# Twelve small loads that nobody reads, on two DMA queues of a decode kernel

## The chip, the cores and the metric

The kernel runs on one core of a Trainium2 chip. The metric is the device time of one execution in microseconds. Three runs of the kernel before gave 188.95 us in the median (188.84 to 189.25).

## The reference

One decode step for a batch of two rows, x of 2 x 448 values in bf16. The rows are normalised, and two branches are added to x: attention over the last 4096 positions of a cache of keys and values (16 query heads, 8 key heads, 256 values a head), and a dense layer with the Mish activation.

```python
xn = layernorm(x)
q  = (xn @ wq)                       # 448 -> 16 heads x 256
k, v = k_cache[:, :, -4096:], v_cache[:, :, -4096:]   # 2 x 8 heads x 4096 x 256 each
p  = softmax(q k^T / 16)
A  = (p v) @ wo                      # 4096 -> 448
h  = xn @ w1 + b1                    # 448 -> 1792
B  = (h * tanh(softplus(h))) @ w2    # 1792 -> 448
out = x + A + B
```

Each key and value is used once for two query heads, so the work is mostly reading: 32 MiB of keys, 32 MiB of values and about 10 MiB of weights.

## The kernel before

The order of all instructions is written out by hand. The cache is worked off in four stages (`u`), each with four of the sixteen (batch, key head) pairs on the 128 partitions, 32 partitions to a pair.

A stage has two loads of k and two of v, 4 MiB each, 128 rows of 32 KB. They share a ring of three buffers with wq, w1 and w2 (`kv_pool`). VectorE turns the keys in blocks (`turns`, line 269), TensorE multiplies them with q (`scores`, line 356), ScalarE takes the exponential (line 364), VectorE turns the weights back (line 367), and TensorE sums the values (`values`, line 402; the last 24 rows of the last load in `values_fixed`, line 435). `finish`, `relay` and `mix` normalise and multiply with wo; `dense_in`, `mish` and `dense_out` are the dense layer, whose second half closes the kernel (`add_rows`, line 249). `pace` is TensorE work whose result is not used.

Every load but one is issued by SyncE, in program order: wq in two halves (line 125), the first two loads of k (line 97), b1 (line 129), w1 (line 500), and then k, v (line 105) and wo (line 111) as buffers come free, and w2 in four parts (line 555). ScalarE issues the load of x (line 118). The store of the result is SyncE's last (line 649). GpSimd issues no DMA: it fills constants (lines 134 to 146), `xs` and the four tiles `sp` (line 281), and has nothing to do after that.

The framework sets the waits. Each DMA of SyncE and ScalarE adds to one of eight completion counters, in turn; a DMA whose counter is in use waits until the earlier DMA on it has landed. DMAs of GpSimd have eight counters of their own. At the end of the program (line 675 in the profile) SyncE waits for the last value of every counter in use, two to an instruction, then all engines meet at a barrier, GpSimd clears the counters, and they meet once more.

Of the kernel before, what the change touches and what calls it, by code (L numbers as in the profile page):

```python
# [11 lines left out]
BF16 = mybir.dt.bfloat16  # L12
# [5 lines left out]
def kernel(  # L18
# [13 lines left out]
    nc = tc.nc  # L32
# [42 lines left out]
    consts = ctx.enter_context(tc.tile_pool(name="consts", bufs=1))  # L75
# [18 lines left out]
    def load_k(u, r):  # L94
        t = ring("k")
        src = kview[u][:, s0:, :].rearrange("j (c t) d -> c j (t d)", c=C)
        nc.sync.dma_start(out=t[:], in_=src[:, :, r * RK * KE : (r + 1) * RK * KE])
        k_t[u, r] = t
# [24 lines left out]
    half = NS * HW // 2  # L123
    for lo in (0, half):
        nc.sync.dma_start(out=wq[:, lo : lo + half], in_=wq_in[:, lo : lo + half])
    wq_t = [wq[:, i * HW : (i + 1) * HW] for i in range(NS)]
    load_k(0, 0)
    load_k(0, 1)
# [10 lines left out]
        out=halves[:], in_=ident[0:2, 0:2].unsqueeze(2).to_broadcast([2, 2, Bsz])  # L139
# [5 lines left out]
    for k in range(KU):  # L145
        nc.gpsimd.tensor_copy(
            out=hot[:, k, :, :, :, k],
            in_=ident[:].rearrange("p (q y) -> p y q", y=4).unsqueeze(2)
# [11 lines left out]
        out=rstd[:], in_=mv[:, 1:2], func=ACT.Sqrt, bias=eps_t[:], scale=1.0  # L160
# [4 lines left out]
        out=xn_bf[:],  # L165
# [8 lines left out]
        out=parm[:], in_=ident[:].rearrange("p (a o) -> p o a", o=2), axis=AXIS.X, op=ALU.add  # L174
# [3 lines left out]
        out=jm[:],  # L178
        in_=ident[:].rearrange("p (a j h) -> p j a h", j=J, h=rep),
# [4 lines left out]
        out=jm[:], in0=jm[:], scalar1=-1.0, scalar2=29952.0, op0=ALU.add, op1=ALU.mult  # L184
# [3 lines left out]
        out=mneg[:], in_=jm[:].unsqueeze(1).to_broadcast([P, TH * 8, J])  # L188
    )
    sel = consts.tile([P, 2, NQ], FP32)  # L190
    for x in range(2):
        for w in range(4):
            at = 32 * w + (2 * (w % 2) + x) * NQ
# [3 lines left out]
            else:  # L197
                nc.vector.tensor_tensor(
                    out=sel[:, x, :], in0=sel[:, x, :], in1=src, op=ALU.add
# [16 lines left out]
    for odd in range(2):  # L216
        for half in range(2):
            o = (half + odd) % 2
            nc.vector.tensor_scalar(
                out=xs[:, odd::2, half * Bsz : (half + 1) * Bsz],  # L220
# [56 lines left out]
    for n in range(2):  # L277
        for e in range(2):
            o = n * 64 + e
            sp = consts.tile([P, G, 32], BF16, name=f"sp{n}{e}")  # L280
            nc.gpsimd.tensor_copy(
                out=sp[:],
                in_=ident[:, o : o + 63 : 2].unsqueeze(1).to_broadcast([P, G, 32]),
            )
            spread[n, e] = sp

    def project():
        q_ps = ps_m.tile([P, 512], FP32, tag="m", name="q_ps")
# [391 lines left out]
```

## Time and profile before

| what | value |
|---|---|
| median of three runs | 188.95 us (188.84 to 189.25) |
| span of the profiled execution | 187.3 us |
| the profiled execution's last record (counters cleared after the program) | 189.25 us after the span's start |
| TensorE busy, weight loads | 84.5 us (45%), 37.4 us (20%) |
| VectorE, ScalarE, GpSimd busy | 92.8 us (50%), 12.4 us (7%), 4.7 us (2%) |
| bytes read, mean rate over the span | 77.67 MB, 415 GB/s |
| mean granted TensorE clock | 0.790 of full speed |

The span runs from the first to the last instruction; the time of a run is longer by what lies around it. A whole time of the profiled execution beside its span is not on the page, so the table has its last record instead.

The DMA view gives packets by queue. q1 is SyncE's queue, q10 ScalarE's, q8 and q14 carry instructions. A packet is one row of a transfer or one completion record of 4 bytes. The profile has the sixteen DMA engines only as a mean; the landing records tell how far apart they finish.

Busy shares are averages over the span. What ends a stage is read from the chain of work that ended last and from the waits.

### The profile page before, as it was taken

Reading aid. Unit: us, or ns where it says so; the run is one execution under the profiler, and the core shown is the slowest. Engines: PE = TensorE matmul, PEld = TensorE weight load, DVE = VectorE, ACT = ScalarE, POOL = GpSimd, SP = SyncE. Lnnn points to the kernel's source line nnn. Section 1 sums busy time; section 2 is a strip of 40 time slices with the busy share of each in tenths; the row PEclk is TensorE's granted clock in tenths of the full one; section 3 lists DMA queues with packets and bytes.
Section 4 is the critical chain, followed back from the end, with each engine's and each line's share of the span. In section 5 each row is a group of like instructions: output and inputs, shape, how many; then the busy total and the mean of one; then the engine's idle time right before and its main releaser. Section 6 shows DMA issues by size and latency. Waiting matters only on the chain.

```text
span 187.3 us, 1938 instructions
## 1 busy us (share of the span) xinstructions
PE 84.5 (45%) x847; PEld 37.4 (20%) x847; DVE 92.8 (50%) x93; ACT 12.4 (7%) x26; POOL 4.7 (2%) x16
## 2 busy tenths in 40 slices
PE   0373015893119000882047002881065068789694
PEld 0211002551003000340012000430021023424353
DVE  6704397974792097038940296048920593040100
ACT  3003000101000100110001000110001000210100
POOL 8100000000000000000000000000000000000000
PEclk9999999955557955599558855698559756999999
DMA  6999999999999999999999999999999999999991
GB/s 215 422 483 427 441 406 408 454 444 448 427 434 413 416 436 406 462 448 441 441 434 402 413 441 422 445 444 434 448 427 420 420 427 434 434 422 408 416 403 45
DMA packets 4195, 77.78 MB, mean 415 GB/s; under 512 B 470, under 2 KB 732, under 8 KB 1628
## 3 DMA queue, kind: packets, MB, share of 16 engines
q1 hardware_dynamic: 4184, 77.67, 97.1%
q8 instruction: 6, 0.10, 0.2%
q14 instruction: 1, 0.01, 0.0%
q10 hardware_dynamic: 4, 0.00, 0.0%
HBM read 77.67 MB, written 0.00 MB: 415 GB/s over the span
## 4 chain that ended last, share of the span: by engine, by line
DMA 64%; DVE 15%; PE 15%; issue 3%; ACT 1%; SPq 1%
DMA v<-in_A_v_cache_dram 32%; DMA k<-in_A_k_cache_dram 15%; DVE kt L269 12%; DMA w<-in_B_w_dram 11%; DMA wq<-in_A_wq_dram 6%; PE pv L402 4%; PE sc L356 3%; PE h_ps L519 2%; DVE p L367 1%; PE acc L249 1%; PE q_ps L291 1%; PE dn L380 1%; DVE rec L388 1%; PE o L435 1%; ACT ex L364 1%
## 5 line engine op out<-in xcount | busy, mean ns | idle before, releaser
L269 DVE STREAM_TRANSPOSE kt<-k 128x4096 f32<-128x4096 f32 x16 | 70.0, 4414 | 33.8 <-DMA k<-in_A_k_cache_dram 33.8
L402 PE MATMUL pv<-v,p 128*32 128x512 bf16 x244 | 22.5, 534 | 59.5 <-DMA v<-in_A_v_cache_dram 59.5
L356 PE MATMUL sc<-kt,qd 128*32 128x512 bf16 x256 | 19.8, 440 | 13.3 <-DVE kt L269 13.3
L402 PEld LDWEIGHTS <-p 128*32 128x32 bf16 x244 | 8.7, 125 | 72.9 <-issue 49.6
L575 PE MATMUL pace<-mneg,ident 128*128 128x512 bf16 x42 | 12.7, 440 | 0.0
L356 PEld LDWEIGHTS <-qd 128*32 128x32 bf16 x256 | 7.1, 104 | 23.5 <-issue 17.5
L447 DVE TENSOR_TENSOR oT<-o,rec 128x16 bf16<-128x16 f32 x4 | 0.7, 174 | 21.3 <-PE o L420 17.6
L367 DVE STREAM_TRANSPOSE p<-ex 128x512 bf16<-128x512 bf16 x8 | 5.2, 690 | 10.8 <-ACT ex L364 10.8
L364 ACT ACTIVATE ex<-sc 128x512 bf16<-128x512 f32 x8 | 4.8, 597 | 86.7 <-PE sc L356 86.7
L388 DVE TENSOR_REDUCE rec<-dn 128x8 f32<-128x512 f32 x4 | 2.8, 691 | 13.3 <-PE dn L380 13.3
L575 PEld LDWEIGHTS <-ident 128*128 128x128 bf16 x43 | 4.2, 111 | 15.1 <-DVE kt L269 9.2
L414 ACT COPY vs<-pv 128x512 f32<-128x512 f32 x4 | 2.3, 586 | 59.5 <-PE pv L402 59.5
L482 PE MATMUL early<-wo,ox 128*2 128x448 bf16 x24 | 5.0, 352 | 1.9 <-ACT ox L473 1.9
L420 PE MATMUL o<-sel,vs 128*128 128x8 f32 x32 | 4.3, 262 | 2.1 <-ACT vs L414 2.1
L420 PEld LDWEIGHTS o<-sel,vs 128*128 128x128 f32 x32 | 4.2, 196 | 4.5 <-ACT vs L414 4.4
L380 PE MATMUL dn<-p,ones 128*128 128x512 bf16 x8 | 2.8, 440 | 3.8 <-DVE p L338 3.8
L575 PE MATMUL pace<-kt,ident 128*128 128x512 bf16 x1 | 0.6, 607 | 8.7 <-DVE kt L269 8.7
L291 PE MATMUL q_ps<-wq,xs 128*32 128x512 bf16 x28 | 3.8, 624 | 1.4 <-DMA wq<-in_A_wq_dram 1.1
L211 PE MATMUL xr_ps<-ident,xrows 2*128 2x2 bf16 x7 | 1.0, 181 | 7.2 <-DVE xrows L210 7.2
L519 PE MATMUL h_ps<-xs,w 128*128 128x4 bf16 x49 | 3.7, 196 | 0.9 <-DMA w<-in_B_w_dram 0.9
L308 DVE COPY qT<-qt_ps 128x16 bf16<-128x16 bf16 x4 | 0.4, 166 | 6.3 <-PE qt_ps L303 6.3
L345 PE MATMUL sc<-mneg,ident 128*128 128x512 bf16 x8 | 3.5, 434 | 0.0
(71 smaller groups left out, 51.7 us busy)
## 6 DMA issues: line engine op xcount, KB each, us to landing
k<-in_A_k_cache_dram SPq DMA_DIRECT2D x8, 4096.0 KB, 27.7
v<-in_A_v_cache_dram SPq DMA_DIRECT2D x7, 4096.0 KB, 21.2
wq<-in_A_wq_dram SPq DMA_DIRECT2D x2, 1792.0 KB, 8.8
wo<-in_A_wo_dram SPq DMA_DIRECT2D x4, 896.0 KB, 19.0
v<-in_A_v_cache_dram SPq DMA_DIRECT2D x1, 2560.0 KB
w<-in_B_w_dram SPq DMA_DIRECT2D x1, 1568.0 KB, 21.2
v<-in_A_v_cache_dram SPq DMA_DIRECT2D x1, 1024.0 KB, 22.2
w<-in_B_w_dram SPq DMA_DIRECT2D x1, 784.0 KB, 23.5
```

What stands on the lines that cost most here:

```text
L269: nc.vector.transpose(out=kt[i][:, :, r, :, :], in_=t[:, r * KE : (r + 1) * KE].bitcast(FP32).rearrange("p (a c j) -> p a c j", c=P // (R ...
L291: nc.tensor.matmul(q_ps[32 * u : 32 * (u + 1), :], lhsT=xs[:, s, :], rhs=wq_t[s][:, u * 512 : (u + 1) * 512], start=(s == 0), stop=(s == N ...
L356: nc.tensor.matmul(sc[32 * w : 32 * (w + 1)].rearrange("p t c m -> p t (c m)"), lhsT=qd[:, u, 2 * n + e, :, :].rearrange("p g q -> p (g q) ...
L364: nc.scalar.activation(out=ex[:, :, :, i, :], in_=sc[:], func=ACT.Exp, scale=scale)
L367: nc.vector.transpose(out=p_all[:, :, h * TH : (h + 1) * TH, :].rearrange("p g t q -> p t g q"), in_=ex[:, h * TH : (h + 1) * TH].rearrang ...
L380: nc.tensor.matmul(dn[:].rearrange("p a q -> p (a q)"), lhsT=ones[:], rhs=p_run[:, i].rearrange("p t q -> p (t q)"), start=(i == 0), stop= ...
L388: nc.vector.tensor_reduce(out=rec[:], in_=dn[:].rearrange("p a q -> p q a"), axis=AXIS.X, op=ALU.add)
L402: nc.tensor.matmul(pv[32 * w : 32 * (w + 1), :, :].rearrange("p x d -> p (x d)"), lhsT=p_run[:, g, 4 * a : 4 * a + 4, :].rearrange("p t q ...
L420: nc.tensor.matmul(po[:, c, :], lhsT=sb[:, x, c::2], rhs=sel[:, x, :], start=(x == 0 and c == 0), stop=(last and x == 1), skip_group_check ...
L482: nc.tensor.matmul(early[:], lhsT=ox[:, i, :], rhs=w[:, i, :], start=False, stop=(u == U - 2 and i == 7),)
L519: nc.tensor.matmul(h_ps[:, i, :, :].rearrange("p k b -> p (k b)"), lhsT=w1_v[:, s, i, :], rhs=xs[:, s, 0 : 2 * Bsz], start=False, stop=(s ...
L575: nc.tensor.matmul(ps[:].rearrange("p t c m -> p (t c m)"), lhsT=ident[:], rhs=rhs, start=True, stop=True, skip_group_check=True,)
```

## The change

A scratch tile `marks` of 16 partitions is added. SyncE loads the first 2, 4, 8 and 12 rows of wo into it, after the two halves of wq and before the first load of k. GpSimd issues eight loads of two rows of wo each, after its last constant. Each load has its own row length, from 256 to 344 values (512 to 688 bytes), and its own place in the tile. Nothing reads the tile.

```diff
     for lo in (0, half):
         nc.sync.dma_start(out=wq[:, lo : lo + half], in_=wq_in[:, lo : lo + half])
+    marks = consts.tile([16, 12, 384], BF16)
+
+    def mark(queue, at, n):
+        w = 256 + 8 * at
+        queue.dma_start(out=marks[0:n, at, 0:w], in_=A_wo[0:n, 0:w])
+
+    for at, n in enumerate((2, 4, 8, 12)):
+        mark(nc.sync, at, n)
     wq_t = [wq[:, i * HW : (i + 1) * HW] for i in range(NS)]
     load_k(0, 0)
...
             spread[n, e] = sp
+
+    for at in range(4, 12):
+        mark(nc.gpsimd, at, 2)
 
     def project():
```

By the built program, the order of the other instructions on every engine stays as it was. The DMAs from the first load of k on take the completion counter four places further in the turn of eight, so the second load of k waits for the landing of x and the load of b1 for that of the first half of wq. The closing waits of SyncE grow from five instructions to nine, because GpSimd's eight counters are now in use; the store's counter, in the fifth and last of them before, is in the fifth of nine.

## The prediction

> **What bounds the kernel now.** I read the DMA view first, then the busy times by stage, the chain of work that ended last, SyncE's waits, and the closing waits of the program (line 675).
>
> ```profile
> DMA  6999999999999999999999999999999999999991
> ...
> q1 hardware_dynamic: 4184, 77.67, 97.1%
> q8 instruction: 6, 0.10, 0.2%
> ...
> q10 hardware_dynamic: 4, 0.00, 0.0%
> ```
>
> Nearly all bytes go over SyncE's queue q1, and the engines are busy in every slice. Six instruction fetches (q8) share them: 0.2% of 16 engines over 187.3 us is 6.0 us, so 1.0 us each, on one engine at a time.
>
> ```profile
> 4.00:12.00 8.00, 3.42 (x26) 1.37 (x30) 4.21 (x25) 0.00 (x0) 1.33 (x6) 1.00 1.03 438
> 12.00:40.00 28.00, 12.53 (x118) 6.67 (x118) 19.57 (x13) 2.66 (x4) 0.00 (x0) 0.96 1.00 433
> ...
> 80.00:160.00 80.00, 32.55 (x320) 12.59 (x319) 41.29 (x24) 4.00 (x10) 0.00 (x0) 0.72 1.01 433
> ...
> 182.00:183.00 1.00, 1.00 (x16) 0.60 (x16) 0.18 (x1) 0.17 (x1) 0.00 (x0) 1.00 0.79 299
> 183.00:184.00 1.00, 1.00 (x26) 0.88 (x24) 0.00 (x0) 0.00 (x0) 0.00 (x0) 1.00 0.36 133
> ```
>
> The last two columns are DMA share and GB/s. The share is 1.00 from 4 us on: the transfers are the bound, and the queue never runs dry. At the end the share falls in steps (0.79, 0.36), since the sixteen engines do not finish together: the completion records of the last weight load lie between 182.64 and 184.59 us.
>
> ```profile
> 157.27 22.25 DMA v<-in_A_v_cache_dram
> 179.51 0.05 issue
> 179.56 0.96 PE o L435 x32
> ...
> 182.41 1.93 PE acc L249 x38
> 184.35 0.02 issue
> 184.37 0.57 PE acc L249 x6
> 184.94 0.37 DVE res L646
> ```
>
> The chain's last stretch: a load of v lands at 179.51, TensorE follows with no slack, the last weights arrive as it needs them (184.59), and the result is ready at 185.3. So a delay of the *slowest* DMA engine moves the end one for one; a delay of a faster one does not.
>
> ```profile
> SPq L649 <- DVE res L646: 16.3, 1, 16.3
> ...
> SPq L675 <- DMA out_dram<-res: 0.6, 1, 0.6
> ```
> ```profile
> L675 SPq EVENT_SEMAPHORE  x4: 28/28/28, 185.7 to 185.9; - x4
> ```
> ```profile
> L675 SPq EVENT_SEMAPHORE  x1: 28/28/28, 186.5 to 186.5; - x1
> ```
>
> After issuing the store of the result (185.37), SyncE runs five waiting instructions, each for two counters. Four pass at once from 185.7 to 185.9, while the store is under way; the fifth holds the store's own counter, waits 0.6 us and passes at 186.5. What follows it (barrier, clearing of counters) ends the span at 187.3.
>
> **The sum's base.** All durations are of the one profiled execution, span 187.3 us. The runs' median is 188.95, 1.65 us more, which is work around the span that the change does not touch; I add the change to 188.95.
>
> **The change part by part.** It removes no work and moves no compute instruction: the order on TensorE, VectorE and ScalarE is the same. It adds twelve loads that nobody reads.
>
> *SyncE's four loads are issued after the two loads of wq, ahead of k.* Issuing a small load took 0.28 us (the store), 0.49 (b1) and 0.53 (x, on ScalarE): four take 1.1 to 2.1, I take 2.0. The two k loads, issued from 1.65 to 2.9, move to about 3.7 to 4.9. The engines are working off wq until its second half lands at 11.88, so 7 us of cover remain: cost nothing. With the cover gone it would cost the 2.0 in full.
>
> *Completion counters.* SyncE and ScalarE's DMAs take eight counters in turn, and a DMA waits for the one eight places before it. Four more DMAs rotate everything from k on by four places. By the built program the second k load now waits for x (landed at 2.0, issue at about 4.3: no wait), and b1's load waits for the first half of wq. That half landed at about 7.6 (the median of the two wq loads is 8.8 and the second took 10.70, so the first took 6.9 from 0.73). Behind b1 on SyncE stands the load of w1, which waits for q_ps until 13.84 anyway; b1 itself is read at 33.9 and sits behind k in the queue (31.3) either way. All later waits name the DMA that they named before. Cost nothing.
>
> *The closing waits: the term I count on.* The same rotation moves the store's counter from the last place to the fifth of nine, since GpSimd's eight counters are added, and their pairing leaves four waiting instructions behind it. The four ahead still pass under the store (185.7 to about 185.95, against 186.5). The four behind are all satisfied, but each has to be run after the store has landed. Four starts from 185.7 to 185.9 are three steps in 0.2 us, 0.065 each: 4 x 0.065 = 0.26 us, on the path. Bounds: 4 x 0.028 (the instruction's own duration) = 0.11, and 4 x 0.07 = 0.28. I take 0.26, because the starts show the full spacing. The clearing of counters that follows (0.096 us for 12) now covers 20: 0 to 0.06, I take 0.03.
>
> *The added transfers.* 26 rows from SyncE (14.2 KB) and 16 from GpSimd (10.1 KB). The trace's packet records give 41 ns for a packet of 896 bytes and 9 ns for a 4-byte completion record. Rows of 512 to 688 bytes lie between; by size 25 to 33 ns. The 470 packets under 512 bytes are 29 large loads with 16 records each and three two-row transfers with 2 each, so a small load uses one engine a row. An engine then gets up to four SyncE rows, 4 x (28 + 9) = 0.15 us, or none, and GpSimd's rows, one each if spread: 32 + 9 = 0.04, with up to eight records 0.10. So 0.04 to 0.25 by engine. Only the slowest engines count. The two that carried b1's rows (and that, if small loads start at the same engines, get most of SyncE's) pass through the middle of the field all along (the records of b1 follow theirs of k), 1 to 1.7 us ahead of the engines that a fetch has held up. I take a middling engine: 1.6 rows x 37 + 41 to 104 ns = 0.10 to 0.16, so 0.13.
>
> The page "DMA: Bandwidth & Descriptors" of the Trainium skill, section "Why a DMA increments its semaphore by 16 and not by 1", says that a load issued from GpSimd posts a completion on all 16 engines whatever its shape. SyncE's two-row b1 posted only 2, so this trace can't show it; by the rule the GpSimd part is 0.10 per engine, by the SyncE row 0.04.
>
> *GpSimd's eight issues.* GpSimd ends its last copy at 5.3 us and does nothing afterwards; no wait follows its loads but the closing ones. No row prices such an issue; the nearest are the issues on the other queues, 0.28 to 0.53, and the copies there, 0.26: eight take 2 to 4 us, done by 10. GpSimd has 175 us to spare.
>
> Sum: 0.26 + 0.03 + 0.13 = 0.42 us, 188.95 + 0.42 = 189.37, rounded to **189.4**, 0.2% up.
>
> **The rivals.** The bound below which this kernel can't be told from no change is 0.2%, 0.38 us; the forecast lies just over it.
>
> *Not slower: the terms stay under the bound.* If the closing waits cost their own duration only (0.11) and the slowest engines get GpSimd's single rows (0.04), the sum is 0.15: 189.1. For it: four satisfied waits may run closer than at 185.7, where the issue of the store stood before them, and engines held up by fetches lead the field by more than any row. It decides as soon as the sum stays under 0.38; against it, the spacing of the waits is read from the same instructions.
>
> *Slower by more: GpSimd's loads hold up something.* VectorE prepares q meanwhile (sel, xrows, xs from 5.5 to 8.9). A delay there has 1.0 us until wq lands (8.9 and 1.9 of matmuls against 11.88), then 3.7 (qd ready at 17.83, k landing at 21.55), then 4.6 before the queue runs dry (w1 lands at 35.0, the next k load was issued at 30.38): 9 us in all. The eight issues as priced stay far inside it. What could reach the stream is a packet of the new queue that stalls its engine for a whole small-load latency, 1.3 us (x: issued at 0.73, landed at 2.03), on an engine that is late: 188.95 + 0.29 + 1.3 = 190.5; half of it, 189.9. Against it: ScalarE's small load shared the engines with wq and its share is 0.0%.
>
> The page "SBUF — State Buffer", section "SBUF: two separate sides", says that a GpSimd operation and some VectorE operations exclude each other on a shared port, for the whole instruction. With about 1 us for each GpSimd issue (the DMA page's first-byte figure) VectorE would lose at most 8 us by this estimate, inside the cover, and the sum stays the same.
>
> *Faster: the late engines change.* The v load that the chain ends with has completion records at 179.24, 179.30 and 179.51. If the added rows shift which engine takes a fetch, the last may fall back on the others: -0.2 to -0.3 on the stream, and with the closing waits at their low bound 188.95 - 0.3 + 0.15 = 188.8. It needs more than 0.38 + 0.29 of gain to be counted as faster; nothing in the profile shows that much.
>
> **How the numbers follow.** Forecast 0.55, under the bound 0.24, GpSimd's loads hold up the stream 0.13, late engines change 0.08. The forecast's terms spread from 0.26 to 0.6; three quarters of it lie above 0.38 (0.42), the rest below (0.13). Slower: 0.42 + 0.13 = 0.55; same: 0.13 + 0.24 = 0.37; faster: 0.08. The range goes from the low end of the faster rival, 188.8, to 190.1, which takes in the milder half of the stall.
>
> **What would show it.** Right: nine waiting instructions at the end of SyncE, the store's wait in the fifth, and 0.25 us from it to the barrier; the chain's landings of v and w no more than 0.25 later; DMA share 1.00 throughout; k issued two microseconds later with wq still landing near 11.9; VectorE's first kt transposes still waiting for k at about 21.6. Wrong: a landing more than 0.5 later, a dip of the DMA share, a wait for GpSimd on any engine, a granted clock under 1.00 in the last 20 us, or a new instruction fetch.

## The result and the profile after

The changed kernel takes 190.11 us, median of five runs (189.73 to 190.38), against 188.95 for the kernel before (188.80 to 189.25) on the same chip. The ratio is 1.0055, 95% interval 1.0037 to 1.0073: slower by 1.04 us by the ratio (0.70 to 1.38), 1.16 by the medians. The forecast was 189.4, and the median lies 0.01 above the upper end of its range. The sign was right; the size was less than half of what came.

The profiled execution of the changed kernel is its quickest run, 189.73 us with a span of 187.9. Wherever a run's time and span are both known, they lie about 1.8 us apart (1.7 to 2.0), before and after, so nothing changed around the span, and the profiled execution of the kernel before (span 187.3) was one of about 189.1. The two traces therefore differ by only 0.6 us, and what follows is read from that smaller difference.

The DMA view of the changed kernel:

```profile
DMA  6999999999999998999999999999999999999990
...
DMA packets 4503, 77.80 MB, mean 414 GB/s; under 512 B 736, under 2 KB 1040, under 8 KB 1936
...
q1 hardware_dynamic: 4236, 77.68, 96.8%
q8 instruction: 6, 0.10, 0.2%
q0 software_dynamic: 256, 0.01, 0.1%
```

A new queue, q0, is GpSimd's. Its eight loads hold 16 rows, but it moved 256 packets: 16 rows and 240 records of 4 bytes. SyncE's q1 has 52 packets more, 26 rows and 26 records. The instruction fetches (q8) are six as before. There is one 8 in the row of the sixteen engines' busy share, near 73 us; at the length of a slice (4.7 us) it can't be told from a 9 that just fell short, and no landing moves there.

The busy times by stage (DMA share and GB/s at the end of each line):

```profile
4.00:12.00 8.00, 3.34 (x22) 1.30 (x23) 3.76 (x23) 0.00 (x0) 5.81 (x14) 1.00 1.05 441
12.00:40.00 28.00, 11.92 (x116) 6.62 (x115) 18.95 (x12) 2.52 (x4) 0.00 (x0) 1.00 1.01 429
...
80.00:160.00 80.00, 39.61 (x324) 15.09 (x324) 41.29 (x24) 3.99 (x10) 0.00 (x0) 0.68 1.00 432
182.00:183.00 1.00, 1.00 (x18) 0.55 (x19) 0.18 (x1) 0.17 (x1) 0.00 (x0) 1.00 0.94 367
183.00:184.00 1.00, 1.00 (x28) 0.90 (x23) 0.00 (x0) 0.00 (x0) 0.00 (x0) 1.00 0.48 183
```

The steady part, 80 to 160 us, moves 432 GB/s against 433: nothing is lost there. 12 to 40 us moves 429 against 433, which over 28 us is 0.26 us of transfer. At the end the engines finish later (share 0.94 and 0.48 where it was 0.79 and 0.36).

The last steps of the chain of work that ended last:

```profile
157.60 22.07 DMA v<-in_A_v_cache_dram
...
179.72 0.96 PE o L446 x32
...
182.72 2.50 PE acc L257 x44
185.22 0.37 DVE res L657
```

It is the same chain, 0.16 us later at the last long load of v (179.67 for 179.51) and 0.28 later at the result, because the last weights land at 184.87 instead of 184.59. The rest of the 0.6 us comes after the result, in the closing instructions (line 686 here, 675 before):

```profile
L686 SPq EVENT_SEMAPHORE  x4: 28/28/28, 186.0 to 186.2; - x4
...
L686 SPq EVENT_SEMAPHORE  x5: 28/28/28, 186.8 to 187.1; - x5
L686 SPq DRAIN  x2: 7/10/13, 187.1 to 187.2; - x2
...
L686 POOLq EVENT_SEMAPHORE_RANGE_CLEAR  x1: 139/139/139, 187.5 to 187.5; - x1
```

Four waits pass while the store is under way. The fifth holds the store's counter, and four more follow it, 0.06 us each: from the store's wait to the drain it is 0.306 us (186.809 to 187.115) where it was 0.065, so 0.24 us on the path. The clearing of the counters took 139 ns, 96 before, and the drain of GpSimd's queue around it 102, 77 before. From the issue of the store to the end of the span it is 0.31 us more.

How the stream came to be later is seen in two views. The timelines of VectorE and SyncE, where the first two transposes of k end and the next load of k is issued, of the kernel before:

```profile
21.58 8.77 DVE L269 STREAM_TRANSPOSE kt<-k 128x4096 f32<-128x4096 f32 x2 [3.75 <-DMA k<-in_A_k_cache_dram]
...
30.38 0.55 SPq L97 DMA_DIRECT2D k<-in_A_k_cache_dram  x1
```

and of the changed kernel:

```profile
22.26 8.77 DVE L277 STREAM_TRANSPOSE kt<-k 128x4096 f32<-128x4096 f32 x2 [4.23 <-DMA k<-in_A_k_cache_dram]
...
31.06 0.55 SPq L97 DMA_DIRECT2D k<-in_A_k_cache_dram  x1
```

The last engine delivers the first k at 22.24 instead of 21.55; VectorE starts 0.68 later and takes as long; the load of k that waits for it is issued 0.68 later. Now the stage from 34 to 38 us, where the loads issued earlier end and this load takes over. Before:

```profile
34.00:38.00 4.00, 3.10 (x42) 2.88 (x41) 4.00 (x2) 0.60 (x1) 0.00 (x0) 1.00 1.09 468
38.00:160.00 122.00, 49.20 (x474) 19.47 (x473) 64.78 (x41) 5.97 (x14) 0.00 (x0) 0.68 1.00 432
```

After:

```profile
34.00:38.00 4.00, 3.10 (x38) 2.31 (x32) 4.00 (x2) 0.60 (x1) 0.00 (x0) 1.00 1.05 434
38.00:160.00 122.00, 56.47 (x483) 22.28 (x481) 65.40 (x41) 5.96 (x14) 0.00 (x0) 0.68 1.00 432
```

468 GB/s became 434, though the share is still above 1.00 (1.05): the engines hold packets, and the packets take longer. By the packet records a packet of 32 KB takes 1.213 us; of those that start between 34 and 36 us some of the changed kernel's take up to 1.62, 2.2 us more in all over the sixteen engines, none in the kernel before. (The rate of so short a stretch is a sign and no measure: kernels without a loss here show 468 to 504. The size is read from the landings.) By the landing records, averaged over the sixteen engines, the load of w1 lands 0.29 us later than before, and the k load behind it 0.56 later. So half of that delay arises at this one place, 10 us after the small loads are done, and from there it stays to 160 us (0.44 to 0.58); the other half is there before, with the first k 0.42 late in the mean. What puts it there is the question of the experiments.

### The profile page after: what moved, and what is told of

Its sections match the earlier page's. It is cut to its first block, busy times and chain, and to the rows that moved or that the text cites. A ratio compares the mean times of both kernels' runs of the same rounds, so it can differ in the third digit from the quotient of the medians.

```text
span 187.9 us, 1954 instructions
## 1 busy us (share of the span) xinstructions
PE 91.3 (49%) x847; PEld 39.6 (21%) x847; DVE 92.3 (49%) x93; ACT 12.4 (7%) x26; POOL 9.1 (5%) x24
## 4 chain that ended last, share of the span: by engine, by line
DMA 63%; PE 16%; DVE 15%; issue 3%; ACT 1%; SPq 1%
DMA v<-in_A_v_cache_dram 31%; DMA k<-in_A_k_cache_dram 15%; DVE kt L277 12%; DMA w<-in_B_w_dram 12%; DMA wq<-in_A_wq_dram 6%; PE pv L413 4%; PE sc L367 3%; PE h_ps L530 2%; DVE p L378 1%; PE acc L257 1%; PE q_ps L302 1%; PE o L431 1%; PE dn L391 1%; PE o L446 1%; DVE rec L399 1%
## 5 line engine op out<-in xcount | busy, mean ns | idle before, releaser
L413 PE MATMUL pv<-v,p 128*32 128x512 bf16 x244 | 23.1, 544 | 53.4 <-DMA v<-in_A_v_cache_dram 53.4
L367 PE MATMUL sc<-kt,qd 128*32 128x512 bf16 x256 | 22.0, 484 | 13.8 <-DVE kt L277 13.8
L367 PEld LDWEIGHTS <-qd 128*32 128x32 bf16 x256 | 7.6, 113 | 26.8 <-issue 22.0
L586 PE MATMUL pace<-mneg,ident 128*128 128x512 bf16 x42 | 12.1, 424 | 0.0
L493 PE MATMUL early<-wo,ox 128*2 128x448 bf16 x24 | 6.5, 426 | 1.9 <-ACT ox L484 1.9
L431 PE MATMUL o<-sel,vs 128*128 128x8 f32 x32 | 5.9, 311 | 2.1 <-ACT vs L425 2.1
L431 PEld LDWEIGHTS o<-sel,vs 128*128 128x128 f32 x32 | 5.7, 261 | 4.5 <-ACT vs L425 4.4
L391 PE MATMUL dn<-p,ones 128*128 128x512 bf16 x8 | 3.3, 499 | 3.4 <-DVE p L349 3.4
L356 PE MATMUL sc<-mneg,ident 128*128 128x512 bf16 x8 | 4.5, 568 | 0.0
L130 POOL DMA_DIRECT2D marks<-in_A_wo_dram x8 | 4.3, 542 | 0.0
## 6 DMA issues: line engine op xcount, KB each, us to landing
w<-in_B_w_dram SPq DMA_DIRECT2D x1, 1568.0 KB, 21.6
w<-in_B_w_dram SPq DMA_DIRECT2D x1, 784.0 KB, 23.8
```

The source lines that it names most:

```text
L367: nc.tensor.matmul(sc[32 * w : 32 * (w + 1)].rearrange("p t c m -> p t (c m)"), lhsT=qd[:, u, 2 * n + e, :, :].rearrange("p g q -> p (g q) ...
L391: nc.tensor.matmul(dn[:].rearrange("p a q -> p (a q)"), lhsT=ones[:], rhs=p_run[:, i].rearrange("p t q -> p (t q)"), start=(i == 0), stop= ...
L413: nc.tensor.matmul(pv[32 * w : 32 * (w + 1), :, :].rearrange("p x d -> p (x d)"), lhsT=p_run[:, g, 4 * a : 4 * a + 4, :].rearrange("p t q ...
L431: nc.tensor.matmul(po[:, c, :], lhsT=sb[:, x, c::2], rhs=sel[:, x, :], start=(x == 0 and c == 0), stop=(last and x == 1), skip_group_check ...
L493: nc.tensor.matmul(early[:], lhsT=ox[:, i, :], rhs=w[:, i, :], start=False, stop=(u == U - 2 and i == 7),)
L586: nc.tensor.matmul(ps[:].rearrange("p t c m -> p (t c m)"), lhsT=ident[:], rhs=rhs, start=True, stop=True, skip_group_check=True,)
```

## The experiments

Each kernel was timed in turns with the kernel before on the same chip, five rounds; the ratio is to that, with its 95% interval. "Field" is the mean landing over the sixteen engines, "next k" the load issued at 30.38 us in the kernel before.

**A copy of the kernel before** (e0). 188.94 us, ratio 1.001 [0.999, 1.003]. Its expectation:

> The kernel before, run once more as a measure of the spread and of what lies between span and time. Both theories: ratio 1.000 within 0.002; spans 186.9 to 187.6 us; time minus span about 1.65 us (the changed kernel's five runs have 1.77 to 1.83). If time minus span is 1.8 here too, the 0.15 between the two kernels outside the span is chance.

Its profiled execution happened to be one of its longer runs, 189.77 us. There the first k landed at 22.02, the next k was issued at 30.84, and 34 to 38 us moved 420 GB/s: the same picture as after the change, with no small load in the kernel. So the kernel before meets this in at least one of its own runs.

**SyncE's four alone** (e1):

```diff
-    for at in range(4, 12):
-        mark(nc.gpsimd, at, 2)
```

> SyncE's four loads alone; GpSimd's eight are left out. The store's counter now stands in the first of five closing waits, with four behind it. Theory A (closing waits plus GpSimd's packets): the store passes in the first wait and the drain follows 0.25 us later than before, landings of the large loads shift by 0.05 us on average, in all +0.30 us, ratio 1.0016. Theory B (SyncE's rows and the later issue of k delay the stream): landings +0.4, in all +0.65, ratio 1.0035.

189.30 us, 1.0026 [1.0015, 1.0037]: +0.49 us by the ratio, and +0.33 by the medians. The interval holds both expectations (1.0016 and 1.0035), so the time does not tell them apart; the profile has to. Its closing waits:

```profile
L684 SPq EVENT_SEMAPHORE  x5: 28/28/28, 186.1 to 186.3; - x5
L684 SPq DRAIN  x2: 7/10/13, 186.4 to 186.4; - x2
```

All five come after the store, since the turn of the counters puts the store's into the first of them: 0.32 us from its passing to the drain (186.06 to 186.38), against 0.065 before. The clearing takes 96 ns as before. The first k landed at 21.78, the next k was issued at 30.60, the field of w1 (34.68) and of the next k (44.46) is within 0.05 us of before. The closing waits make 0.26 us of the rise. In this profile SyncE's rows cost the stream next to nothing; but it is of the quickest of twelve runs (188.92), and what the other 0.1 to 0.2 us of the median is, no profile shows.

**GpSimd's eight alone** (e2):

```diff
-    for at, n in enumerate((2, 4, 8, 12)):
-        mark(nc.sync, at, n)
```

> GpSimd's eight loads alone; SyncE's four are left out. Nine closing waits, the store's counter in the last: nothing behind it. Theory A: no change from the store's landing to the drain, +0.04 for the clearing of 20 counters instead of 12, landings of the large loads +0.4 to +0.5 on average from 44 us on, in all +0.5 to +0.7, ratio 1.003 to 1.004. Theory B: landings +0.05, ratio 1.0005.

189.95 us, 1.0054 [1.0042, 1.0067], as slow as the whole change and slower than either view expected. The profile is of its longest run (190.27). Its closing waits, the last of nine and what follows:

```profile
L684 SPq EVENT_SEMAPHORE  x1: 28/28/28, 187.6 to 187.6; - x1
L684 SPq DRAIN  x2: 7/7/7, 187.7 to 187.7; - x2
```

Here the store's counter is last, so no wait is left behind it, and the end costs 0.07 us at most. The rise lies in the stream:

```profile
34.00:38.00 4.00, 3.29 (x41) 2.52 (x36) 4.00 (x2) 0.60 (x1) 0.00 (x0) 1.00 1.00 396
```

The first k landed at 22.19, the next k was issued at 31.02, and the stage moved 396 GB/s (468 before). From w1 to the next k the field took 10.31 us, 9.76 before. So GpSimd's loads bring the delay of the stream. SyncE's shift the store's counter ahead of other waits, and so bring the delay at the end.

**SyncE's four issued twice** (e3), to double their price:

```diff
+    for at, n in enumerate((2, 4, 8, 12)):
+        mark(nc.sync, 12 + at, n)
```

> The changed kernel with SyncE's four loads issued twice (into other places of the tile), so that the counters turn by eight and the store's counter is again in the last of nine closing waits. Theory A: 0.25 us less than the changed kernel at the end, 0.06 more for the four extra loads: about 0.2 us under it, ratio 1.0045 to the kernel before. Theory B: the rows cost twice, landings +0.8 to +0.9, ratio 1.006 or more.

193.13 us, 1.0244 [1.0205, 1.0284]. Nobody expected this. SyncE's waits and its timeline:

```profile
SPq L130 <- DMA wq<-in_A_wq_dram: 8.4, 2, 4.5
```
```profile
1.66 10.94 SPq L130 DMA_DIRECT2D marks<-in_A_wo_dram  x8
12.64 1.27 SPq L97 DMA_DIRECT2D k<-in_A_k_cache_dram  x2
```

The seventh and eighth small loads take the completion counters of the two wq loads and wait until these have landed; k stands behind them and is issued at 12.64 instead of 3.00. The stage then ran dry:

```profile
12.00:16.00 4.00, 2.50 (x18) 0.83 (x17) 0.42 (x4) 1.73 (x2) 0.00 (x0) 1.00 0.58 199
```

Every later landing is about 3.7 us late. The experiment says nothing of the rows' price. It does show what the turn of eight counters costs when a load falls on one that is still under way. In the change itself that place falls to the load of b1, behind both loads of k.

**More and fewer of GpSimd's packets** (e4, e5). Sixteen of its loads in place of eight, and one load of 16 rows with SyncE's four removed:

```diff
-    for at in range(4, 12):
+    for at in range(4, 20):
```

> The changed kernel with sixteen loads by GpSimd instead of eight. Theory C: k's first landing sees the same eight or so before it, the second eight lie behind it and add 0.1 us of packets: ratio 1.0055 to 1.007. Theory D: GpSimd's share doubles, ratio 1.009 to 1.010.

```diff
-    for at in range(4, 12):
-        mark(nc.gpsimd, at, 2)
+    nc.gpsimd.dma_start(out=marks[0:16, 4, 0:288], in_=A_wo[0:16, 0:288])
```

> Nothing of SyncE's four; GpSimd issues one load of sixteen rows instead of eight of two rows: as many rows, one completion per engine instead of eight. Theory C with the cost by number of packets: 32 packets instead of 256, k's first landing and the later issue as in the kernel before, ratio 1.000 to 1.001. Theory D with a cost for the mere use of the queue: 1.003 or more.

Sixteen loads: 190.08 us, 1.0053 [1.0041, 1.0065], no more than eight; the next k was issued at 31.05, as with eight. One load: 189.04, 1.0008 [0.9995, 1.002], no change that can be told. So the cost of the whole does not grow from eight loads to sixteen, as it would if each packet took its own share of the path. The landing records show how: with sixteen the field of w1 is later itself (35.15 us, 34.94 with eight), so that at the issue of the next k more of it was left, and the next k landed at 45.00, as with eight (44.97). The two delays did not add up there. The profile of the one load is of its longest run (190.11 us), in which the next k was issued at 30.91.

**The issue of k made late by other means** (f3). The kernel before, without any small load; two copies on VectorE between the first two transposes (0.84 us together):

```diff
+            if (u, i, r) == (0, 0, 1):
+                for n in range(2):
+                    nc.vector.tensor_copy(
+                        out=hold[:], in_=jm[:].unsqueeze(1).to_broadcast([P, TH * 8, J])
+                    )
```

> The kernel before with two copies of 0.46 us each on VectorE between the first two turns of the first keys; no load and no wait is added. Every buffer release by these turns, and so the issue of the first load of k after w1, comes 0.92 us later (31.3 instead of 30.4 us). Theory C: rate dips between 34 and 38 us, all later landings 0.7 to 1.2 us later, ratio 1.004 to 1.006. Theory D: w1 lands at 35.0, so a load issued at 31.3 is still ahead of it by 3.7 us: ratio 1.000.

190.26 us, 1.0060 [1.0043, 1.0077]. The issue of k and its stage:

```profile
31.41 0.55 SPq L97 DMA_DIRECT2D k<-in_A_k_cache_dram  x1
```
```profile
34.00:38.00 4.00, 3.77 (x46) 2.74 (x39) 4.00 (x2) 0.60 (x1) 0.00 (x0) 1.00 1.08 435
```

Every load up to w1 landed as before (field within 0.01); the k load issued 1.0 us later landed 0.35 later in the field and 1.14 later on its last engine, with packets of 32 KB 3.1 us too long in all between 34 and 36 us. That is as much as the whole change costs, made by a late issue alone, if by a later one (1.0 us against 0.68). When k was issued, w1 still had 3.2 us to run in the field.

**The same late issue with other work queued ahead** (f4), and that work alone (f1): the first load of wo goes right behind w1, and is left out at its own place.

```diff
+    load_wo(0)
...
-        load_wo(u)
+        if u > 0:
+            load_wo(u)
```

> The two copies on VectorE and the early load of wo together. Theory C: k is issued at 31.3, but the queue now holds 2.1 us more ahead of it, so the delay is covered: no dip, ratio 0.998 to 1.001. Theory D: 1.000. If the delay costs here too, what it costs is not the queue running out but VectorE's own work.

> The kernel before with the first load of wo (0.9 MB, 2.1 us of the queue) issued right behind w1 instead of behind the second load of v; nothing added. Theory C (the loss of the changed kernel comes where w1 ends and the next load of k was issued late: the engines run out of reads although the load was issued some 4 us ahead): k is now issued with 2 us more cover, landings of k 2.1 us later and all else as before, ratio 0.998 to 1.000, fewer runs above 189.3 us. Theory D (GpSimd's packets themselves or the late engines cost it): 1.000.

f4: 189.00 us, 1.0014 [0.9993, 1.0034], with k issued at 31.45, as late as in f3:

```profile
34.00:38.00 4.00, 3.88 (x48) 2.85 (x41) 4.00 (x2) 0.60 (x1) 0.00 (x0) 1.00 1.18 504
```

f1: 189.05 us, 1.0005 [0.9993, 1.0016]. With the issue late, the work queued ahead takes the loss away; without a late issue it gains nothing. f3, f4 and f1 ran on one chip, and the intervals of f3 and f4 don't meet. So this loss is one of a queue that has too little ahead when the next load is issued.

**The same cover in the changed kernel** (f2):

> The changed kernel with the same early load of wo. Theory C: the loss at the end of w1 goes (0.3 to 0.5 us); what stays are the closing waits 0.26, the clearing of counters 0.07 and the packets 0.1 to 0.3, in all 0.4 to 0.6 us over the kernel before, ratio 1.002 to 1.003. Theory D: 1.0055 as without the early load.

189.43 us, 1.0036 [1.0015, 1.0057]; by the medians 0.45 us over before, and 0.68 less than the changed kernel without it, which was timed on another chip. The issue of k (31.15) is as late as after the change, and the stage is whole:

```profile
34.00:38.00 4.00, 3.09 (x38) 2.21 (x32) 4.00 (x2) 0.60 (x1) 0.00 (x0) 1.00 1.16 494
```

Four of its twelve runs took 190.3 to 191.0, so that its interval is wide and overlaps that of the changed kernel: f2 agrees with f3 and f4, and would not settle it without them. Its profile is of one of the four (190.26), and shows the same loss at a second place. A load of v, issued at 95.60 us in the kernel before, comes much later in f2:

```profile
95.60 0.54 SPq L105 DMA_DIRECT2D v<-in_A_v_cache_dram  x1
```
```profile
102.17 0.54 SPq L105 DMA_DIRECT2D v<-in_A_v_cache_dram  x1
```

The load of k ahead of it then had 3.03 us to run in the field, and the v behind took 10.00 us. In g2 below (profile of a run of 190.44 us) it was 3.31 and 10.24. In the twelve other profiles 4.08 us or more were left there (9.31 in the kernel before), and the v took 9.67 to 9.70. The load waits for two transposes on VectorE, which began at 93.42 instead of 86.86; why they did is not shown.

**GpSimd's eight loads later** (g1), alone, held behind a copy of `act_bf` on GpSimd, so that they are issued from 41.6 us on instead of 5.5:

```diff
+    hold = consts.tile([P, NI, 2, Bsz], BF16)
+    nc.gpsimd.tensor_copy(out=hold[:], in_=act_bf[:])
+    for at in range(4, 12):
+        mark(nc.gpsimd, at, 2)
```

> GpSimd's eight loads alone, as in the run without SyncE's four, but held back on GpSimd by one small copy that reads the dense layer's activations, so that they start after 41 us, when the first load of k behind w1 has long been issued. Theory C (their cost is that they make k's first landing, and with it that issue, late): issue at 30.4 to 30.8, no dip from 34 to 38 us; what stays is the clearing of 20 counters, 0.07, and 0.1 for the packets, ratio 1.001. Theory D (the use of GpSimd's queue costs, whenever it is): 1.004 to 1.0055.

189.12 us, 1.0003 [0.9982, 1.0023]; against e2's interval (1.0042 to 1.0067) the same eight loads at another time bring no change that can be told. The first k landed at 21.72, the next k was issued at 30.54:

```profile
34.00:38.00 4.00, 3.09 (x42) 2.79 (x40) 4.00 (x2) 0.60 (x1) 0.00 (x0) 1.00 1.14 490
```

**The store's counter put last** (g2): f2 with four more of SyncE's small loads behind wo, so that the turn of the counters ends with the store's in the ninth wait.

> The changed kernel with the early load of wo and four more small loads of SyncE behind it, so that the counters turn by eight and the store's counter is again in the last of nine closing waits. Both theories: 0.065 us from the store's wait to the drain instead of 0.31, so 0.25 us under the changed kernel with the early load, plus 0.06 for the new rows: about 0.2 under it, ratio to the kernel before 1.0015 to 1.002.

189.10 us, 1.0024 [1.0004, 1.0044]; the median is 0.33 under f2's (on another chip), though the four loads were added. Its last wait and what follows it:

```profile
L690 SPq EVENT_SEMAPHORE  x1: 28/28/28, 187.8 to 187.8; - x1
L690 SPq DRAIN  x2: 7/10/13, 187.9 to 187.9; - x2
```

From the store's wait to the drain it is 0.065 us (187.789 to 187.854), in f2 0.306 (187.340 to 187.646). The intervals of the two ratios overlap (four of the twelve runs of each were over 190), so the 0.24 us is shown by the traces, and the medians only agree with it.

## Why the prediction was right in sign and wrong in size

| Term | predicted | shown by |
|---|---|---|
| closing waits behind the store | 0.26 us | 0.24 in the profile after; e1, g2 |
| clearing of 20 counters | 0.03 | 0.07 (clear +43 ns, drain +25) |
| the stream of transfers | 0.13 | 0.28 in the profile after, its quickest run; 1.04 - 0.31 = about 0.7 over the runs; e2, f3, f4 |
| issue of SyncE's four, turn of counters | 0 | no wait in the profile after; e1 leaves 0.1 to 0.2 open |

*The closing waits: right.* Nine waits, the store's in the fifth, four behind it at 0.06 us. e1, where the turn of the counters sets four behind the store for another reason, shows the same size.

*The clearing: low by 0.04*, above the 0.06 that was given as its upper bound. The bound counted the clearing instruction alone; the drain of GpSimd's queue next to it grew as well.

*SyncE's issues and the rotated counters: right, as far as the profile shows.* From the timeline of SyncE, and its wait for b1's counter:

```profile
1.65 1.31 SPq L130 DMA_DIRECT2D marks<-in_A_wo_dram  x4
3.00 1.25 SPq L97 DMA_DIRECT2D k<-in_A_k_cache_dram  x2
```
```profile
SPq L137 <- DMA wq<-in_A_wq_dram: 3.5, 1, 3.5
```

Four issues took 1.31 us, not 2.0; k followed at 3.00, under wq, which landed at 12.08. b1 waited 3.5 us for the first half of wq, and w1 behind it was issued at 14.05 anyway (13.84 before).

*The added transfers: this step failed*, and in it the sentence on cover: a delay of VectorE "has 1.0 us until wq lands ..., then 3.7 ..., then 4.6 before the queue runs dry (w1 lands at 35.0, the next k load was issued at 30.38): 9 us in all". The first two figures are not in dispute, but they cover VectorE and not k: a first k that lands late itself has only the last of the three. And the 4.6 us was taken as slack, as if a load might be issued until the moment the queue ends. The runs show it isn't. Ordered by the time from the issue of the next k to the field's landing of w1, for all kernels that have only w1 ahead of it:

| kernel | issue of next k, us | lead to w1, us | from w1 to next k in the field, us |
|---|---|---|---|
| e3, SyncE's eight | 34.01 | 4.30 | 9.82 |
| before | 30.38 | 4.26 | 9.76 |
| e4, sixteen of GpSimd's | 31.05 | 4.10 | 9.85 |
| e1, SyncE's four | 30.60 | 4.08 | 9.78 |
| g1, GpSimd's late | 30.54 | 4.07 | 9.76 |
| after | 31.06 | 3.88 | 10.03 |
| e0, long run of a copy of before | 30.84 | 3.85 | 10.13 |
| e5, one of GpSimd's, its longest run | 30.91 | 3.83 | 9.90 |
| e2, GpSimd's eight | 31.02 | 3.75 | 10.31 |
| f3, late by VectorE | 31.41 | 3.24 | 10.11 |

With a lead of 4.07 us or more at most 0.09 us is lost in the field, with 3.88 or less 0.14 to 0.55, and on the last engine more (1.14 in f3, 1.50 in e2). The size does not follow the lead evenly; each row is one execution. The second place, with f2 and g2, has the same border: 3.03 and 3.31 us lost 0.33 and 0.57, and 4.08 or more at most 0.03. So the 4.26 us of the kernel before, taken to the field, held some 0.2 to 0.4 us of cover, and not the 4.6.

The small packets were priced rightly one by one: nearly all rows have 27 to 34 ns in the packet records and every 4-byte record of GpSimd's queue 9, priced at 25 to 33 and 9. But there were more records than priced, and in the field they came to more than 0.13 us: w1 was 0.29 us late after the change (0.12 in e2, 0.03 in e1). And they made the slowest engine's part of the first k late: 22.19 to 22.33 us in four profiles with GpSimd's eight or sixteen loads early, and 22.76 in g2, where kernels without small loads of GpSimd before it have 21.55 to 21.83 (e0's long run 22.02, e3 with its late k left out). VectorE waits for that slowest engine, so the chain ran: late last engine, late transposes, late issue, thin queue. The prediction priced only the first link, and called the others covered.

*That only the slowest engine counts: right at the end, and misleading here.* It matters at every load that an engine waits for, and here the wait set an issue that all sixteen engines need.

*GpSimd's records: the higher of the two figures was nearer.* The page "DMA: Bandwidth & Descriptors" of the Trainium skill, section "Why a DMA increments its semaphore by 16 and not by 1", has a completion on all sixteen engines for a load from GpSimd. The 256 packets of q0 agree: 30 records of 4 bytes a load. Sixteen of them fit the completions; the fourteen others are as many as the engines without a row (e5's one load of sixteen rows has sixteen records). That is 15 records an engine and not the eight that were priced.

*No delay of VectorE by GpSimd's issues: right.*

```profile
5.54 4.27 POOL L130 DMA_DIRECT2D marks<-in_A_wo_dram  x8
```

Eight issues took 4.27 us, 0.54 each, while VectorE prepared q; its last step for that (xs) began at 7.78 us, 8.26 before. The port that the page "SBUF — State Buffer" of the Trainium skill, section "SBUF: two separate sides", describes as shared did not show here.

*The rivals.* "Slower by more" gave 189.9 to 190.5 and the time falls there, but its mechanism did not happen: no packet stalled its engine for 1.3 us, and the longest small row of the profile after took 0.14. That the range reached to 190.1, and so almost to the time, came from half of that stall: the nearness is luck. The rival's other half, a late VectorE, did happen, through the late k and not through GpSimd's issues, and was set aside by the 9 us of cover. "Under the bound" fell with the spacing of the closing waits. "Late engines change" is not seen: the last long load of v landed 0.16 us later, not earlier.

*The signs.* Nine waits, the time from the store's wait and wq near 11.9 (12.08) came as named, and the end of the chain nearly so (0.16 and 0.28 later, for at most 0.25). The first kt transposes did not (22.26 for 21.6), and one of the signs of being wrong came: landings more than 0.5 us later, 0.69 at the first k and 0.56 in the field of the next. It points at the step that failed.

*What stays open.* Why the lead has to be about 4 us was not shown. How so few records delay the slowest engine by 0.4 us and more was not shown either, nor why both sets together cost the field of the first k more (0.42 us after the change, 0.47 in f2) than the sum of each alone (0.05 in e1, 0.14 in e2). The traces are of single executions, and the profile after accounts for 0.6 of the 1.04 us; that the other runs lose the rest at the same place is an inference from e2, whose profile was of a longer run, and f3. Of the single runs over 190 us, only the profiled ones of f2 and g2 show a place (the second one above) and e5's part of a cause (0.14 us in the table); the others, in f2, f4, g1, g2, the copy of before (190.97) and the kernel before itself (190.88), have no profile. No version was measurably quicker than the kernel before.

## What to carry to other kernels

A busy queue is no measure of slack: take a load's cover from its issue to the end of the work queued ahead, and subtract the lead that the queue needs, about 4 us at the two places seen here. A small load is priced by the wait that it delays, not by its bytes, so look for the next instruction that waits for the slowest engine and for what is issued behind that wait. And count the completion counters: how many waits stand behind the last store, and which load comes eight places later.

## What the runs showed of the hardware that was not expected

- An issue lead of 3.88 us or less before the queue's end cost 0.14 to 0.57 us in the field at two places of the kernel, 4.07 or more at most 0.09. At the first place the DMA share from 34 to 38 us was 1.00 or above in every profile read there, and only the GB/s (468 before, 396 in e2) and the length of single packets (1.213 us, up to 2.37 in f3) showed it.
- A two-row load from GpSimd moves 32 packets: 2 rows and 30 records of 4 bytes. Beside packets of 32 KB (1.213 us each) such loads landed 2.4 us apart in e2, which at about two small packets to an engine is one for one, so that in the changed kernel eight loads issued by 9.8 us landed until 23.8 us.
- The seventh small load on SyncE waited for the landing of the load eight places before it; two such waits, 8.4 us together, made the kernel 2.4% slower.
- Eight more counters in use cost 0.24 us in waits (0.06 for two counters) where they stand behind the store, and 0.07 us of clearing wherever they stand.
